# Linear attention into a gated MLP on one core: W_out staged as fp32 on SyncE's queue, half of W_in moved behind step 2, and a new hand-written order

## The chip, the cores and the metric

One core of one Trainium2 chip runs the kernel; the others are idle. The metric is the device time of one execution in microseconds, as a median of several runs. TensorE is called PE here (PEld is its loading of weights), VectorE DVE, ScalarE ACT, GpSimd POOL, and SyncE SP; SP issues nearly all DMAs, all on one queue.

## What is computed

The inputs are q, k and v of shape (4 batches, 8 heads, 768 tokens, 64), a decay per head, and the weights of a gated MLP. All are fp32, and so is the output (4, 768, 512).

```
for each block of 64 tokens b:                      # causal linear attention with decay lam
    out[b]  = (q_b k_b^T * Dmask) v_b + (q_b * lam^(i+1)) @ kv_state
    kv_state = lam^64 * kv_state + (k_b * lam^(63-i))^T v_b
x = out as (batch, token, 512)
h = relu(x @ w_in); u, v = halves of h              # w_in 512 x 1024
v = (v - mean(v)) / sqrt(var(v) + 1e-6)
v = w_spatial @ v + b_spatial                       # mixes the 768 tokens of a batch
y = (u * v) @ w_out                                 # w_out 512 x 512
```

## The kernel before, in words

**Tiles.** The 4 x 768 tokens are cut into 12 steps of 256 tokens, numbered n = 0 to 11, three to a batch. A step is two tiles c = 0, 1 of 128 tokens. Everything on PE is bf16 with fp32 sums in PSUM, of which eight banks are used: seven for work, and bank 7 for the running state of the attention. q, k and v are loaded as fp32 into three buffers each (512 KB a load), the decays are multiplied in while they are turned into bf16 (`qc`, `kc`, two buffers each), and v is cast (`vb`, two buffers). In steps 0 to 4 PE transposes qc and kc and an engine copies the result out of PSUM; from step 5 on SP does it with DMA transposes.

**Order.** The kernel is written as one list of tokens, `ORDER` (L16 to L85). Each token is an operation with its arguments and, last, its engine: T is PE, D is DVE, A is ACT, P is POOL, S is SP. `tc.manual_schedule()` (L570) takes them as they stand, so each engine executes its own tokens strictly in that order, and semaphores between engines follow from the data. A token that waits holds all later tokens of its engine. Engines that appear in the text are therefore a part of the token: `QM.2.0.D` is on DVE and `QM.2.0.P` on POOL. The tokens that the text uses:

| token | what | line |
|---|---|---|
| LQ, LK, LV n | SP loads q, k, v of step n | L195 |
| QM, KM n.x | decay times q or k, half x of the heads' pairs | L316 |
| VC n, VD n.x | cast of v, whole or half | L184 (POOL), L180 (ACT), L182 (DVE) |
| TQ, TK / EQ, EK | PE transposes of q, k / their copy out of PSUM | L351 / L180, L182 |
| DQ, DK n | the same by DMA transpose from SP | L333, L329 |
| SC n.i, MK n.i | scores, half i / times the causal mask | L381, L386 |
| KV n.c, SS n.c | add to the state / copy it out | L398, L180 or L182 |
| AV n.c | attention output of part c (state part and block part) | L419, L428 |
| FN n | one-element read of a bank after AV n.0 | L441 by copy |
| EX n.z | copy of the attention output to xT | L180, L182 |
| PV n.c, EV n.c, BN n.c | x @ w_in for the v half / relu / mean and variance | L453, L458 or L460, L468 and L469 |
| RA, RD, RB, VN | 1/sqrt(var) and the normalising of v | L473, L478, L483, L489 or L492 |
| PU n.j, EU n.j | x @ w_in for the u half / relu | L504, L458 or L460 |
| WT k.i, EW k.i | PE transposes of w_spatial, rows' half i / copy out | L516, L180 or L182 |
| GP, PW, GM b.f.i | bias into a bank / spatial product of batch b / times u | L526, L530, L536 |
| PO b.t, EO, ST | product with w_out, copy out, store of a 128 x 512 tile | L541, copy, L564 |
| PH, EH, SH | the same for half a tile, used for the last one | L550, copy, L560 |
| FL k.w | k matmuls of width w on ones, whose result nobody reads | L299 |

**Stages.** The start holds steps 0 to 2 up to PU, and then WT; for batch b, eight PW need all of the batch's normalised v, and are followed by its six PO, mixed with the attention and the first MLP product of the next batch. GN (L496) is a one-element copy on POOL that only waits for VN 2.1 (and VN 5.0), so that POOL's later tokens start after it.

**Weights.** WH.0 and WH.1 load the v half of w_in as fp32 into the staging buffer `wst[0]`, WH.2 and WH.3 the u half into `wst[1]`; CW.0 to 3 and CX.0 and 1 cast them to bf16. WQ.0 to 5 load the six row blocks of w_spatial (384 KB each) into parts of `wst[0]`, `wss` and `wst[1]`, once the casts have read what was there; WC casts them. WO (L279) is one DMA from POOL's own queue that loads w_out and casts it on the way.

Of the kernel before, what the change touches and what calls it, by code (L numbers as in the profile page):

```python
# [8 lines left out]
FP32 = mybir.dt.float32  # L9
# [7 lines left out]
msk.P one.D idn.P FL.6.256.3.1.T LQ.0.S lam.A BR.A tab.0.A row.D LK.0.S FL.2.256.2.1.T LK.1.S LB.6.T LQ.1.S  # L17
FL.16.128.0.1.T LV.0.S WH.0.S WH.1.S LV.1.S WH.2.S LQ.2.S LK.2.S WH.3.S LV.2.S FL.6.256.2.0.T posk.P mkc.D
LN.6.A LL.D LX.A tab.1.A QM.0.1.D QM.0.0.P KM.0.0.P KM.0.1.D TQ.0.0.3.T TQ.0.1.5.T EQ.0.0.3.D TK.0.0.4.T
EQ.0.1.5.A EK.0.0.4.A KM.1.0.D TK.0.1.0.T BB.1.2.T KM.1.1.D EK.0.1.0.D BE.1.2.A QM.1.0.D SC.0.0.5.6.T TK.1.1.1.T  # L20
FL.2.256.2.0.T SC.0.1.3.4.T TK.1.0.0.T EK.1.1.1.A MK.0.0.5.6.D EK.1.0.0.A TQ.1.0.2.T EQ.1.0.2.A MK.0.1.3.4.D
VC.0.P BB.0.1.T BE.0.1.A KV.0.0.T QM.1.1.P SC.1.0.5.6.T SS.0.0.A MK.1.0.5.6.D AV.0.0.3.4.T FN.0.3.4.A TQ.1.1.2.T
KV.0.1.T EQ.1.1.2.A AV.0.1.3.4.T SS.0.1.A CW.0.P CW.1.P CW.2.P CW.3.P WQ.0.S WQ.1.S WQ.2.S WQ.3.S SC.1.1.0.1.T
eps.D EX.0.0.3.D EX.0.1.4.A MK.1.1.0.1.D VD.1.0.A VD.1.1.P PV.0.0.2.T EV.0.0.2.D PV.0.1.5.T EV.0.1.5.D KV.1.0.T
SS.1.0.A AV.1.0.0.1.T FN.1.0.1.A KV.1.1.T AV.1.1.0.1.T SS.1.1.A BN.0.0.D CX.0.P EX.1.0.0.D EX.1.1.1.A PU.0.0.5.T
EU.0.0.5.A PV.1.0.6.T QM.2.1.P BN.0.1.D QM.2.0.D RA.0.A EV.1.0.6.A TQ.2.1.3.T EQ.2.1.3.A KM.2.0.D PV.1.1.2.T
EV.1.1.2.A TQ.2.0.4.T EQ.2.0.4.A KM.2.1.D TK.2.0.0.T TK.2.1.1.T PU.1.0.5.T EK.2.0.0.D EK.2.1.1.D BN.1.0.D RD.0.D
EU.1.0.5.A CX.1.P WQ.4.S WQ.5.S LQ.3.S LK.3.S LV.3.S SC.2.0.3.4.T SC.2.1.0.1.T PU.0.1.6.T MK.2.0.3.4.D VC.2.P
EU.0.1.6.A MK.2.1.0.1.D RB.0.D KV.2.0.T SS.2.0.A PU.1.1.5.T AV.2.0.3.4.T FN.2.3.4.A EU.1.1.5.A BN.1.1.D
AV.2.1.3.4.T WC.0.P WC.1.P WC.2.P WT.0.0.6.T EX.2.1.4.A EX.2.0.3.D WT.1.0.2.T WT.2.0.0.T EW.0.0.6.D EW.1.0.2.A  # L30
RA.1.A EW.2.0.0.D VN.0.0.D LQ.4.S LK.4.S PV.2.0.1.T EV.2.0.1.A BN.2.0.D PV.2.1.4.T EV.2.1.4.A VN.0.1.A BN.2.1.D
RD.1.D VN.1.0.D VN.1.1.D WC.3.P WC.4.P WC.5.P QM.3.1.P GP.0.0.0.4.A RA.2.A GP.0.2.0.5.A PU.2.0.3.T EU.2.0.3.A
PU.2.1.0.T EU.2.1.0.A WT.0.1.6.T WT.1.1.2.T RD.2.D VN.2.0.D VN.2.1.D EW.0.1.6.D WT.2.1.1.T EW.1.1.2.D EW.2.1.1.D
LV.4.S LQ.5.S LK.5.S GN.2.1.P QM.3.0.P KM.3.1.P KM.3.0.P PW.0.0.0.4.T GP.0.3.1.3.A PW.0.2.0.5.T TQ.3.2.6.T
GM.0.0.0.4.D GP.0.1.0.0.A EQ.3.2.6.A PW.0.3.1.3.T PW.0.1.0.0.T TK.3.2.1.T GP.0.3.0.4.A PW.0.3.0.4.T GM.0.2.0.5.D
GM.0.3.1.3.D GM.0.1.0.0.D EK.3.2.1.D VC.3.A SC.3.0.1.2.T SC.3.1.5.6.T QM.4.0.P QM.4.1.P KM.4.0.P KV.3.0.T
# [52 lines left out]
def kernel(  # L89
# [514 lines left out]
```

## Time and profile before

| | us |
|---|---|
| median of 3 runs | 143.67 (143.55 to 143.78) |
| profiled execution, first to last instruction (span) | 148.0 |
| PE, DVE, ACT, POOL busy in it | 136.3, 113.5, 76.3, 58.1 |

The profile is one execution of its own, taken by the hardware profiler; its only time is its span, and that is longer than the runs without it. Times below are microseconds from the start of that span. PE's busy time is that of pipelined matmuls with modelled ends, so 10 busy microseconds in 10 do not mean that PE streams at its full rate: the rate is read from how far apart groups of matmuls start. The chain of waits follows the work back from the last instruction, at each step to whatever released it; its pieces give start, duration, engine, tile, line and count.

### The profile page before, as it was taken

To read this page: it belongs to the slowest core of one execution; us is meant where nothing else is said; L and a number is where in the kernel's file an instruction comes from. 1 tells how busy PE (TensorE), PEld (TensorE's weight loads), DVE (VectorE), ACT (ScalarE), POOL (GpSimd) and SP (SyncE) were. 2 spreads that over 40 slices of the span, in tenths; PEclk is the share of its full clock that TensorE was granted. 3 is DMA by queue.
4 is the path that set the end of the run, shared out by engine and by line. 5 is a ranking of instruction groups with operands and counts; after the bars stand their busy time and mean duration, and the time that the engine had idled before them with its cause. 6 is when DMAs were issued, how large, how long until landed. Compare 5 with 4: busy or idle time off the path is not lost.

```text
span 148.0 us, 4675 instructions
## 1 busy us (share of the span) xinstructions
PE 136.3 (92%) x1965; PEld 87.4 (59%) x1983; DVE 113.5 (77%) x220; ACT 76.3 (52%) x155; POOL 58.1 (39%) x67
## 2 busy tenths in 40 slices
PE   5979999599999979999999999999999999999990
PEld 3846645377767636565766564776664655856540
DVE  3484669997978858679599959986898989984930
ACT  3564618247973434676921476778508443480040
POOL 5529537970299924398510504904700000000000
PEclk9985579999999999999999999999999999999998
DMA  3999999999969999999898399999987550510174
GB/s 89 346 355 371 352 357 406 367 303 330 326 190 275 125 130 293 334 217 296 184 273 83 80 303 373 241 320 235 198 180 102 190 213 30 187 71 0 39 300 159
DMA packets 58841, 34.12 MB, mean 231 GB/s; under 512 B 15939, under 2 KB 54595, under 8 KB 58820
## 3 DMA queue, kind: packets, MB, share of 16 engines
q1 hardware_dynamic: 58144, 33.17, 82.2%
q0 software_dynamic: 528, 0.52, 2.7%
q8 instruction: 15, 0.25, 0.7%
q10 hardware_dynamic: 148, 0.13, 0.3%
q14 instruction: 6, 0.05, 0.1%
HBM read 24.38 MB, written 6.29 MB: 207 GB/s over the span
## 4 chain that ended last, share of the span: by engine, by line
PE 78%; DVE 8%; ACT 4%; DMA 3%; issue 3%; POOL 2%; POOLq 0%
PE ps L530 20%; PE ps L504 13%; PE ps L453 13%; PE ps L541 13%; PE ps L398 4%; PE ps L381 4%; PE ps L428 4%; DMA q_in<-in_q_dram 3%; PE ps L351 3%; DVE a_sb L386 2%; PE ps L419 2%; DVE kc L316 2%; PE ps L285 2%; PE ps L516 1%; DVE gT L536 1%
## 5 line engine op out<-in xcount | busy, mean ns | idle before, releaser
L386 DVE TENSOR_TENSOR a_sb<-ps,m 128x1024 bf16<-128x1024 f32 x24 | 28.9, 1218 | 6.9 <-PE ps L381 4.5
L530 PE MATMUL ps<-wt_sb,vn 128*128 128x384 bf16 x192 | 33.8, 326 | 0.2 <-ACT ps L180 0.2
L530 PEld LDWEIGHTS <-vn 128*128 128x128 bf16 x192 | 18.2, 98 | 12.5 <-issue 0.4
L316 POOL TENSOR_TENSOR kc<-k_in,lv 128x512 bf16<-128x512 f32 x16 | 17.4, 1097 | 20.4 <-DMA k_in<-in_k_dram 8.3
L453 PE MATMUL ps<-win_sb,xT 128*128 128x512 bf16 x87 | 22.8, 393 | 1.0 <-DVE xT L182 0.4
L504 PE MATMUL ps<-xT,win_sb 128*128 128x256 bf16 x192 | 23.5, 273 | 0.0
L316 POOL TENSOR_TENSOR qc<-q_in,lqn 128x512 bf16<-128x512 f32 x19 | 20.4, 1090 | 4.6 <-DMA q_in<-in_q_dram 4.5
L536 DVE TENSOR_TENSOR gT<-ps,uT 128x384 bf16<-128x384 f32 x32 | 16.8, 550 | 6.9 <-PE ps L530 3.8
L541 PE MATMUL ps<-wout_sb,gT 128*128 128x512 bf16 x83 | 21.2, 379 | 0.7 <-issue 0.5
L504 PEld LDWEIGHTS <-win_sb 128*128 128x128 bf16 x192 | 18.1, 98 | 3.9
L468 DVE BATCH_NORM_STATS2 st<-vh 128x6 f32<-128x512 bf16 x24 | 16.3, 681 | 1.5 <-ACT vh L458 1.4
L458 ACT ACTIVATE vh<-ps 128x512 bf16<-128x512 f32 x19 | 11.4, 598 | 9.2 <-PE ps L453 9.2
L180 ACT ACTIVATE o_sb<-ps 128x512 f32<-128x512 f32 (+1 forms) x17 | 9.6, 570 | 12.2 <-DVE o_sb L182 8.9
L453 PEld LDWEIGHTS <-xT 128*128 128x128 bf16 x96 | 9.2, 101 | 10.9 <-issue 1.4
L541 PEld LDWEIGHTS <-gT 128*128 128x128 bf16 x92 | 8.6, 98 | 9.0 <-DVE gT L536 0.2
L458 ACT ACTIVATE uT<-ps 128x512 bf16<-128x512 f32 x17 | 9.8, 588 | 5.0 <-PE ps L504 5.0
L398 PEld LDWEIGHTS <-kc 64*64 64x64 bf16 x320 | 7.1, 113 | 7.2 <-issue 5.6
L180 ACT ACTIVATE ps<-bsp 128x384 f32<-128x384 f32 x21 | 10.0, 488 | 2.4 <-DVE a_sb L386 1.2
L428 PE MATMUL ps<-a_sb,vb 64*64 64x128 bf16 x384 | 11.2, 225 | 0.0
L180 ACT ACTIVATE xT<-ps 128x512 bf16<-128x512 f32 x16 | 9.1, 594 | 4.1 <-PE ps L428 3.9
L184 POOL CAST vb<-v_in 128x1024 bf16<-128x1024 f32 (+1 forms) x7 | 6.8, 976 | 10.7 <-DMA v_in<-in_v_dram 5.5
L180 ACT ACTIVATE s_sb<-ps 128x256 bf16<-128x256 f32 x15 | 5.7, 380 | 10.3 <-PE ps L398 10.2
(69 smaller groups left out, 181.8 us busy)
## 6 DMA issues: line engine op xcount, KB each, us to landing
q_in<-in_q_dram SPq DMA_DIRECT2D x12, 512.0 KB, 7.0
k_in<-in_k_dram SPq DMA_DIRECT2D x12, 512.0 KB, 6.1
v_in<-in_v_dram SPq DMA_DIRECT2D x12, 512.0 KB, 6.1
out_dram<-o_sb SPq DMA_DIRECT2D x23, 256.0 KB, 2.6
wst<-in_moe_w_in_dram SPq DMA_DIRECT2D x4, 512.0 KB, 6.6
wst<-in_moe_w_spatial_dram SPq DMA_DIRECT2D x4, 384.0 KB, 6.1
wss<-in_moe_w_spatial_dram SPq DMA_DIRECT2D x2, 384.0 KB, 6.3
wout_sb<-in_moe_w_out_dram POOLq DMA_DIRECT2D x1, 512.0 KB, 5.9
```

What stands on the lines that cost most here:

```text
L180: nc.scalar.activation(out=o, in_=i, func=AF.Copy)
L316: vec(e).tensor_tensor(out=dst[n % NCA][:, u].rearrange("p u m o d -> p o (u m) d"), in0=src[n % NIN].rearrange("p (o u) m d -> p o u m d" ...
L386: nc.vector.tensor_tensor(out=a_sb[n % NA][:, i].rearrange("p o w j x -> p o w (j x)"), in0=ps[:, b0:b1 + 1:b1 - b0].rearrange("p o (w y) ...
L398: nc.tensor.matmul(out=pkv[row(o), u], lhsT=kc[n % NCA][row(c), u, m, o, :], rhs=vb[n % NCA][row(c), 4 * o + u, m, :], start=new and u == ...
L428: nc.tensor.matmul(out=po[c ^ o][row(w), c, i], lhsT=vb[n % NCA][row(c), 4 * o + u, j, :], rhs=a[row(c), i, o, w, j, :], start=(r == 0 and ...
L453: nc.tensor.matmul(out=bank(b), lhsT=x[:, slot(c, g)], rhs=win_sb[:, g, DH:DFF], start=(g == 0), stop=(g == NCH - 1))
L458: nc.scalar.activation(out=o, in_=i, func=AF.Relu)
L468: nc.vector.bn_stats(out=st6[p2][:, t], in_=vh[p2][:, t])
L504: nc.tensor.matmul(out=pu[:, f2].rearrange("p (c x) -> p c x", c=2), lhsT=win_sb[:, g, f * P:(f + 1) * P], rhs=x[:, slot(0, g):slot(1, g) ...
L530: nc.tensor.matmul(out=bank(b)[:, 0:HW], lhsT=vn[bb % 2][:, s, f * P:(f + 1) * P], rhs=wt_sb[:, s, i * HW:(i + 1) * HW], start=False, stop ...
L536: nc.vector.tensor_tensor(out=gT[bb % 2][:, f, cols], in0=bank(b)[:, 0:HW], in1=uT[bb % 2][:, f, cols], op=ALU.mult)
L541: nc.tensor.matmul(out=bank(b), lhsT=gT[bb % 2][:, f, t * P:(t + 1) * P], rhs=wout_sb[:, f, :], start=(f == 0), stop=(f == NCH - 1))
```

## The change

Three things change at once.

1. **w_out** is no longer loaded by POOL's queue. SP loads it as fp32 (1 MB) into `wst[0]` behind step 4's keys (`WP`), and POOL casts it in two instructions of 128 x 1024 (`WX.0`, `WX.1`).
2. **The u half of w_in** (`WH.2`, `WH.3`) is loaded behind step 2's q and k, no longer WH.2 ahead of them and WH.3 behind them. The row blocks of w_spatial come in the order 2, 1, 0, 3, 5, 4.
3. **All orders are new**, and many tokens change their engine. `brow`, the bias row, is now the first row of `bsp`. The new functions for a state kept in two banks (`KP`, `SX`, `SY`, `SA`), `FX` and `BQ` are not used by the new order.

```diff
-    brow = sb([1, S], FP32, "brow")
+    brow = bsp[0:1]
...
+    def w_p(e):
+        nc.sync.dma_start(out=wst[0], in_=moe_w_out.rearrange("(t p) f -> p t f", p=P))
+
+    def w_x(e, j):
+        copy(e, wout_sb[:, 2 * j:2 * j + 2], wst[0][:, 2 * j:2 * j + 2])
```

The start of the order, engine by engine, before (-) and after (+), fillers left out of DVE and ACT:

```diff
-SP   LQ.0 LK.0 LK.1 LQ.1 LV.0 WH.0 WH.1 LV.1 WH.2 LQ.2 LK.2 WH.3 LV.2 WQ.0 .. WQ.5 LQ.3 LK.3 LV.3 LQ.4 LK.4 LV.4 LQ.5 LK.5 LV.5 LK.6 LV.6 DQ.5 DK.5
+SP   LQ.0 LK.0 LK.1 LQ.1 LV.0 WH.0 WH.1 LV.1 LQ.2 LK.2 WH.2 WH.3 LV.2 WQ.2 WQ.1 WQ.0 WQ.3 WQ.5 WQ.4 LQ.3 LK.3 LV.3 LQ.4 LK.4 WP LV.4 LK.5 LQ.5 LK.6 LV.5 DK.5 DQ.5
-POOL QM.0.0 KM.0.0 VC.0 QM.1.1 CW.0 CW.1 CW.2 CW.3 VD.1.1 CX.0 QM.2.1 CX.1 VC.2 WC.0 .. WC.5 QM.3.1 GN.2.1 QM.3.0 KM.3.1 KM.3.0 QM.4.0 QM.4.1 KM.4.0 KM.4.1 WO QM.5.1 QM.5.0 KM.5.0 KM.5.1 VC.4 KM.6.0
+POOL QM.0.0 KM.0.0 KM.1.0 QM.1.0 QM.1.1 KM.1.1 CW.3 CW.2 QM.2.0 KM.2.1 KM.2.0 CX.1 VC.2 WC.2 WC.1 WC.5 WC.4 QM.3.1 GN.2.1 KM.3.1 VC.3 QM.4.1 QM.4.0 KM.4.1 KM.4.0 WX.0 WX.1 VC.4 QM.5.0 QM.5.1 KM.6.1
-DVE  QM.0.1 KM.0.1 EQ.0.0 KM.1.0 KM.1.1 EK.0.1 QM.1.0 MK.0.0 MK.0.1 MK.1.0 EX.0.0 MK.1.1 EV.0.0 EV.0.1 BN.0.0 EX.1.0 BN.0.1 QM.2.0 KM.2.0 KM.2.1 EK.2.0 EK.2.1 BN.1.0 RD.0 MK.2.0 MK.2.1 RB.0 BN.1.1 EX.2.0 EW.0.0
+DVE  QM.0.1 KM.0.1 EQ.0.0 EK.0.1 BE.0 EQ.0.1 MK.0.0 MK.0.1 EK.1.0 CW.1 SS.0.0 FN.0 EQ.1.0 BE.1 EX.0.1 MK.1.0 MK.1.1 EV.0.1 BN.0.1 QM.2.1 EV.0.0 BN.0.0 EK.2.0 MK.2.1 EV.1.0 MK.2.0 BN.1.1 BN.1.0 FN.2 RD.0 WC.0 RB.0
-ACT  EQ.0.1 EK.0.0 BE.1 EK.1.1 EK.1.0 EQ.1.0 BE.0 SS.0.0 FN.0 EQ.1.1 SS.0.1 EX.0.1 VD.1.0 SS.1.0 FN.1 SS.1.1 EX.1.1 EU.0.0 RA.0 EV.1.0 EQ.2.1 EV.1.1 EQ.2.0 EU.1.0 EU.0.1 SS.2.0 FN.2 EU.1.1 EX.2.1
+ACT  EK.0.0 VC.0 EQ.1.1 CW.0 EK.1.1 EX.0.0 SS.0.1 VD.1.1 VD.1.0 SS.1.0 FN.1 EX.1.0 EX.1.1 EQ.2.0 EQ.2.1 EK.2.1 CX.0 EV.1.1 RA.0 SS.1.1 EU.1.1 SS.2.0 EU.1.0 EU.0.0 RA.1 EX.2.0 EX.2.1 EU.0.1
-PE   .. PV.0.0 PV.0.1 KV.1.0 AV.1.0 KV.1.1 AV.1.1 PU.0.0 PV.1.0 TQ.2.1 PV.1.1 TQ.2.0 TK.2.0 TK.2.1 PU.1.0 SC.2.0 SC.2.1 PU.0.1 KV.2.0 PU.1.1 AV.2.0 AV.2.1 WT.0.0 WT.1.0 WT.2.0
+PE   .. PV.0.0 PV.0.1 KV.1.0 AV.1.0 AV.1.1 TQ.2.0 PV.1.0 TQ.2.1 TK.2.1 PV.1.1 TK.2.0 SC.2.1 KV.1.1 SC.2.0 PU.1.0 PU.0.0 PU.1.1 KV.2.0 AV.2.0 PU.0.1 AV.2.1 WT.1.0 WT.2.0 WT.0.0
```

From the first WT to the first PW of batch 1, DVE has 61 tokens after and 56 before; among them the decays KM.3.0, QM.3.0, KM.5.0, KM.5.1, KM.6.0 (before: QM.6.1 and KM.8.0). Batch 0's first PO stands ahead of step 3's PV after, and behind step 4's first AV before. The end of the order:

```diff
-PE   PW.3 x7 PO.3.0 PW.3.3.1 PO.3.2 PO.3.4 PO.3.1 PO.3.3 PH.3.5.0 PH.3.5.1
+PE   PW.3 x8 PO.3.1 PH.3.5.1 PH.3.5.0 PO.3.2 PO.3.3 PO.3.4 PO.3.0
```

The last copy and store are that of half a tile before, and of a whole tile (`EO.3.0` on ACT, `ST.3.0` on SP) after.

More of the change, by code (lines that the diff above doesn't have):

```diff
@@ L16 @@
 ORDER = """
[L17 to L36, printed above, removed]
@@ L82 @@
[L82 to L84 removed]
+LQ.0.S LK.0.S LK.1.S LQ.1.S LV.0.S WH.0.S WH.1.S LV.1.S posk.P msk.P idn.P row.D one.D lam.A BR.A tab.0.A
+FL.6.256.1.1.T FL.2.256.3.1.T FL.2.256.3.1.T LB.5.T FL.16.128.3.1.T FL.6.256.4.1.T mkc.D LN.5.A LL.D LX.A QM.0.1.D
+QM.0.0.P TQ.0.0.5.T KM.0.1.D TK.0.1.3.T EQ.0.0.5.D EK.0.1.3.D KM.0.0.P BB.0.0.T TK.0.0.5.T TQ.0.1.1.T KM.1.0.P
@@ L172 @@
     wss = sb([P, 2, S], FP32, "wss")
+    ysb = many(2, [P, 4 * D], FP32, "ysb") if " KP." in ORDER else None
     wst = many(2, [P, NCH, DH], FP32, "wst")
@@ L299, in f_l, with f_x @@
             nc.tensor.matmul(out=bank(b)[:, 0:w], lhsT=ones[:, 0:P], rhs=ones[:, 0:w],
+                             start=(new == 1 and i == 0), stop=True, skip_group_check=True)
+    def f_x(e, k, w, new):
+        for i in range(k):
+            nc.tensor.matmul(out=bank(SB)[:, 4 * D:4 * D + w], lhsT=ones[:, 0:P], rhs=ones[:, 0:w],
                              start=(new == 1 and i == 0), stop=True, skip_group_check=True)
```

137 lines of the change are left out of this document (87 added, 50 removed).

## The prediction

> **What bounds the kernel now.** I read the page first, then a table by stages, then the timeline of the start.
>
> ```profile
> span 148.0 us, 4675 instructions
> PEclk9985579999999999999999999999999999999998
> PE 78%; DVE 8%; ACT 4%; DMA 3%; issue 3%; POOL 2%; POOLq 0%
> ```
>
> The chain that ends last is PE for 78% of 148.0. The other 22% is where time can be found. The table by stages (columns: stretch, length, busy PE, PEld, DVE, ACT, POOL with counts, granted clock, DMA share, GB/s) tells where it lies:
>
> ```profile
> 6.80:10.20 3.40, 2.55 (x40) 1.64 (x39) 3.02 (x6) 1.62 (x3) 1.42 (x1) 1.00 1.15 346
> 10.20:20.40 10.20, 9.62 (x145) 5.83 (x144) 5.95 (x8) 4.85 (x11) 6.96 (x9) 0.50 1.10 362
> 20.40:33.50 13.10, 10.84 (x234) 7.33 (x233) 11.87 (x20) 6.59 (x15) 9.12 (x9) 1.00 1.04 355
> 33.50:72.50 39.00, 37.27 (x583) 24.99 (x580) 31.33 (x65) 24.86 (x51) 23.37 (x25) 1.00 1.08 248
> 72.50:100.90 28.40, 28.14 (x451) 17.97 (x453) 23.48 (x48) 16.27 (x35) 9.02 (x9) 1.00 0.96 237
> 100.90:130.40 29.50, 29.02 (x426) 18.22 (x429) 26.57 (x53) 14.90 (x32) 4.53 (x4) 1.00 0.62 159
> ```
>
> From 33.5 on PE is idle for little: 1.7, 0.3 and 0.5 in the three stretches. What PE has to stream there does not change, and takes these pieces of the chain (start, length, engine, line, count):
>
> ```profile
> 39.24 1.95 PE ps L530 x12
> ...
> 72.92 3.90 PE ps L530 x24
> ...
> 84.05 3.45 PE ps L541 x16
> ...
> 89.96 2.59 PE ps L453 x12
> ...
> 97.65 3.49 PE ps L504 x32
> ...
> 115.39 0.45 PE ps L381 x32
> ...
> 130.75 6.99 PE ps L530 x42
> ```
>
> So a PW costs 0.98 (1.95 for two), a PO 0.86, a PV 0.86, a PU 0.87, a score half 0.22. Batch 1's first PW stands near 72.5, batch 3's near 130.4. Ahead of 33.5 it is otherwise: the clock is 0.50 from 10.2 to 20.4, and from 20.4 to 33.5 DVE is busy for 11.87 of 13.10 while the queue moves 355 GB/s. That is the stage of this change, and its timeline says which wait ends last:
>
> ```profile
> 5.14 0.69 DVE L316 TENSOR_TENSOR qc<-q_in,lqn 128x512 bf16<-128x512 f32 x1 [0.68 <-DMA q_in<-in_q_dram]
> ...
> 17.77 1.04 POOL L184 CAST win_sb<-wst 128x1024 bf16<-128x1024 f32 x1 [0.51 <-DMA wst<-in_moe_w_in_dram]
> ...
> 17.97 1.89 PE L453 MATMUL ps<-win_sb,xT 128*128 128x512 bf16 x4 [0.37 <-DVE xT L182]
> ...
> 19.28 1.04 POOL L316 TENSOR_TENSOR qc<-q_in,lqn 128x512 bf16<-128x512 f32 x1 [0.47 <-DMA q_in<-in_q_dram]
> ...
> 22.08 1.04 POOL L184 CAST win_sb<-wst 128x1024 bf16<-128x1024 f32 x1 [1.76 <-DMA wst<-in_moe_w_in_dram]
> ...
> 24.13 1.04 POOL L184 CAST vb<-v_in 128x1024 bf16<-128x1024 f32 x1 [1.01 <-DMA v_in<-in_v_dram]
> ...
> 24.16 1.55 DVE L316 TENSOR_TENSOR qc<-q_in,lqn 128x512 bf16<-128x512 f32 x1
> ...
> 25.64 2.53 DVE L316 TENSOR_TENSOR kc<-k_in,lv 128x512 bf16<-128x512 f32 x2
> ...
> 27.00 0.40 PE L351 MATMUL ps<-ident,kc 128*128 128x128 bf16 x4 [0.83 <-DVE kc L316]
> ...
> 28.23 0.40 PE L351 MATMUL ps<-ident,kc 128*128 128x128 bf16 x4 [0.83 <-DVE kc L316]
> ...
> 28.46 1.04 PE L504 MATMUL ps<-xT,win_sb 128*128 128x256 bf16 x8
> ...
> 33.58 1.18 PE L516 MATMUL ps<-ident,wsp_raw 128*128 128x128 bf16 x18
> ```
>
> Step 2's three decays on DVE run from 24.16 to 28.17, though q had landed by 19.28. PE waits for each (0.83, 0.83), and steps on only at 28.46. Beside POOL's casts such a decay takes 1.27 to 1.55, alone 0.69 (at 5.14).
>
> **The change part by part.** Durations that I need besides:
>
> ```profile
> L316 POOL TENSOR_TENSOR kc<-k_in,lv 128x512 bf16<-128x512 f32 x16 | 17.4, 1097 | 20.4 <-DMA k_in<-in_k_dram 8.3
> L386 DVE TENSOR_TENSOR a_sb<-ps,m 128x1024 bf16<-128x1024 f32 x24 | 28.9, 1218 | 6.9 <-PE ps L381 4.5
> L180 ACT ACTIVATE xT<-ps 128x512 bf16<-128x512 f32 x16 | 9.1, 594 | 4.1 <-PE ps L428 3.9
> L180 ACT ACTIVATE vb<-v_in 128x1024 bf16<-128x1024 f32 x3 | 3.2, 1050 | 0.0
> L468 DVE BATCH_NORM_STATS2 st<-vh 128x6 f32<-128x512 bf16 x24 | 16.3, 681 | 1.5 <-ACT vh L458 1.4
> ```
>
> *Queue.* From WH.2 (17.77) to q 2 (19.28) a 512 KB load takes 1.5. With both u quarters behind step 2's q and k, q 2 is usable at 17.8, k 2 at 19.3, the first quarter at 20.8, the second and v 2 at 22.1 and 24.1 as before.
>
> *Steps 0 and 1.* v 0 is cast on ACT, so POOL takes step 1's keys and queries. Both score halves of step 0 stand together, and their masks follow back to back on DVE (1.22 each, from about 10.1 to 12.5; before there is a gap). I get the end of AV.0.1 at 14.7 and the first PV at 16.0, 2.0 ahead of 17.97. At half clock a PV takes about 1.7: both end at 19.4. Then KV, AV, a state copy and AV: 20.9. Now something else is late: both EX of step 1 are on ACT, 0.59 each one behind the other, so PV.1.0 waits till 22.25.
>
> *Step 2.* Three of four decays are on POOL at 1.1: 17.8 to 18.9, 19.3 to 21.5; the fourth is on DVE behind step 0's statistics, done at 22.6 if it takes as long as at 24.16. The transposes therefore interleave with PV.1.0 and PV.1.1 and end at 24.7, not 28.6. Scores: 24.75 and 25.5.
>
> *u half.* `CX.0` sits on ACT behind EK.2.1, from 24.6 for 1.05 (the row of vb, same size): the first PU starts at 25.7, not after a landing. From there four PU (3.9 with their edges), KV (16 matmuls) and AV (48), 0.9 by the score halves' 0.22 for 16, give 30.5. `WC.0` is on DVE behind two statistics (0.9 each with their sum) and the read that waits for AV.2.0.
>
> ```profile
> L182 DVE CAST vb<-v_in 128x1024 bf16<-128x1024 f32 x2 | 1.5, 744 | 0.0
> ...
> L182 DVE COPY qT<-ps 128x512 bf16<-128x512 bf16 x1 | 0.4, 425 | 0.0
> ```
>
> DVE has no cast of 128x768 in the trace. From below it is bounded by the copy of 512 columns, 0.42, from above by the decay beside POOL, 1.55; I take 0.7, since the cast of 1024 at 0.74 is the nearest row. Done at 30.95, so **WT starts at 31.0 instead of 33.58: -2.6.**
>
> *First WT to batch 1's first PW.* PE has three WT, 2 PV, 2 PU, three WT (5.7 in all), then 30.5 to batch 1's first PW. I walked all four engines through it and find waits of 1.85: 0.2 for the bias copy of the third PW behind QM.3.0, 0.2 before SC.3.0, 0.25 where `KM.5.1` and `KM.5.0` stand ahead of MK.4.1, 0.55 where MK.5 comes behind `KM.6.0`, 0.4 for both EX of step 5 on ACT, 0.25 in smaller ones. That is 38.05. Before it took 39.0 with 0.2 more PE work in it: **-0.7.** DVE does not bound it: its 56 operations before sum to 34.5 at their mean durations and show 31.33 busy, because neighbours overlap; the 61 after sum to 37.7, by the same ratio 34.2, under PE's 36.2. (The heavy kinds are alike: 6 MK, 8 GM, 8 statistics, 9 VN. What differs is 5 decays for 2 and 3 relus of v for none, against 2 EW for 5.)
>
> *w_out.* What goes is one issue on POOL:
>
> ```profile
> L279 POOL DMA_DIRECT2D wout_sb<-in_moe_w_out_dram x1 | 0.9, 931 | 0.0
> ```
>
> WP takes 3.0 (twice a 512 KB load). After v 2 (24.1) come six w_spatial blocks (384 KB, 1.1 each) and five inputs (1.5 each), 38.2, so w_out is usable at 41.2, or 42.3 if WQ.5 has to wait for `CX.0` on ACT. POOL reaches `WX` at 43.5 and needs 2 x 1.04. The first PO then comes at 48.8, so 3.3 of cover; the POOL issue that goes was not on the path. What WP delays on SP (v 4, k 5, q 5, k 6, v 5) is usable at 44.9 (v 4), 46.5 (k 5), 48.1 (q 5); k 5 is wanted by DVE at 48.5. Cost 0; if the queue were 2 later, DVE's MK.4.1 behind KM.5 would pay it one for one.
>
> *DMA transposes.* DK.5 can be issued when KM.5.0 is done, 50.5. Landing takes 4.0:
>
> ```profile
> kT<-kc SPq DMA_TRANSPOSE x7, 4.0
> ```
>
> DQ.5 follows it, 57 to 58, and step 5's scores come at 58.3. Further on DK.8 and DQ.8 stand behind KV.6.1, which the new order moves behind five PW; they land between 1.0 ahead of the scores of step 8 and 1.2 behind. I take **+0.3** for both.
>
> *Batches 1 to 3.* From batch 1's first PW to batch 3's PE does the same work but for the 0.2; I find 1.3 of waits, as there are now (57.8 for 56.5): **0**, bounds -0.5 and +1.2.
>
> *Tail.* Before, the last work is two half copies and stores; after, a whole tile.
>
> ```profile
> 143.03 0.97 PE ps L550 x8
> 144.02 0.38 ACT o_sb L180
> ```
>
> A whole copy is 0.2 longer (0.59 to 0.38), a 256 KB store 0.4 longer than one of 128 KB at the loads' rate, and of the two half copies one waits for the other now, which goes: **+0.5.**
>
> Sum: -2.6 - 0.7 + 0.3 + 0 + 0.5 = -2.5. The profiled span would be 145.5. The span lies 4.3 above the median, in both kernels alike as I suppose; so 143.67 - 2.5 = **141.2**.
>
> **The rivals.** *B, the clock returns one window sooner.* The table has the clock at 0.50 for 10.2, three times 3.4, so it is decided by stretches of 3.4. If 13.6 to 17.0, where PE now starts PV.0.0, counts as busy, both PV end at 18.2, not 19.4, and WT starts at 29.5. Time 139.8.
>
> *C, the clock falls once more.* From 6.8 to 10.2 PE is busy 2.55 of 3.40, and the next stretch is at 0.50. From 20.4 to 23.8 the new order has, by my walk, about 2.3 busy, with the wait for PV.1.0 in it. At half clock the 3.0 of PE work in the next 3.4 would cost 2.5. Time 143.7. The Trainium skill, "TensorE: Matmul & The Clock Gate", section "What's actually happening", has the gate decided by free-running windows of about 3.4 us, half rate after an idle one and full after a busy one. The trace agrees with the length (10.2 in three); where "busy" begins, no row here shows.
>
> *D, DVE becomes the bound (slower).* POOL and DVE hold each other up: 1.27 to 1.55 against 0.69 for one decay. After, five decays sit on DVE in the stage from WT to batch 1, beside POOL's own, before two. If operations there do not overlap, the 37.7 and 2.5 to 3 of waits make 40.7 instead of 38.05, and batches 2 and 3, with the same mixture, give 0.6 each more: +2.7 + 1.2 on top of 141.2, **145.1**. It decides once DVE's work in the stage is over PE's 36.2. Against it: 31.33 busy for 34.5. The Trainium skill, "SBUF — State Buffer", section "Who interferes with whom", makes the port pair that DVE and GpSimd share an exclusive lock when a DVE operation has two SBUF inputs; the decays have, and 1.55 against 0.69 agrees with it.
>
> *E, no gain.* WT waits for w_spatial anyway: if the last block is late because WQ.5 must wait for `CX.0` on ACT (25.6), the rest of the queue shifts by 1 and the start's gain is lost in POOL and DVE later. 143.7.
>
> **How the numbers follow.** Forecast 0.50, B 0.15, C 0.13, D 0.17, E 0.05. The forecast's own spread is 1.0 either way. The range runs from 139.3, just under B, to 145.1, half of D. A measurement of this kernel tells about 0.2% from no change, 143.4 to 144.0: that takes half of C and most of E, 0.09. Slower is D and the upper edge of E and C, 0.19. Faster is the rest, 0.72.
>
> **What would show it.** Right: the first w_spatial transposes on PE near 31, batch 1's first PW near 69, batch 3's near 127.5; PE waits for kc of step 2 gone; the first PV near 16. B and C: the granted clock between 10 and 27. D: DVE busy over 34 between WT and batch 1, and PE's waits there for a_sb and kc. Wrong: a wait of PE for w_out, or POOL's `WX` waiting for a landing past 46; a later first PW of batch 1 than 72.5.

## The result and the profile after

| | us |
|---|---|
| before, median of 4 runs beside it | 143.72 (143.55 to 143.94) |
| after, median of 4 runs | 151.4 (148.91 to 155.41) |
| ratio, 95% interval | 1.042 (1.034 to 1.051) |
| profiled execution of after: time, span | 155.41, 153.7 |

The change made the kernel 4% slower where the prediction had it 1.7% faster, and its runs differ by 6.5 where those of before differ by 0.4. Ratios here and below leave out the runs marked slow on record: of after 148.91 and 151.01 count, while the median of all four lies 5% above before. The page of after (span, two rows of the 40 slices, granted clock, GB/s, and the chain of waits by engine):

```profile
span 153.7 us, 4672 instructions
PE   5989989989500999999999999999999999999991
DVE  3569787999999799698787998999489789876850
PEclk9995699999995699999999999999999999999999
GB/s 106 344 368 364 348 342 355 344 315 341 364 183 0 196 83 4 148 293 344 336 186 223 210 129 275 348 317 217 239 240 76 85 303 302 6 0 273 0 203 207
PE 78%; DVE 17%; issue 2%; ACT 1%; DVEq 0%
```

The twelfth and thirteenth slice of PE (42 to 50) are empty, which no slice of before was but the very last; DVE is at 9 (tenths busy) in them; from there on the DMAs move little for five slices (183, 0, 196, 83, 4), and the clock drops to 0.5 a second time. DVE's share of the chain went from 8% to 17%. One wait is behind it (PE's two longest waits for another engine between 30 and 79: engine, line, waited for, total, times, longest):

```profile
PE ps L363 <- DVE kc L328: 9.4, 1, 9.4
PE ps L541 <- DVE vh L497: 0.8, 1, 0.8
```

The timeline from 37.5 on, all engines (start, length, engine, line, operation, tiles, shapes, count, idle time ahead):

```profile
37.54 0.68 DVE L328 TENSOR_TENSOR qc<-q_in,lqn 128x512 bf16<-128x512 f32 x1
37.69 0.58 POOL L533 CAST seen<-vn 1x1 f32<-1x1 bf16 x1 [4.78 <-DVE vn L529]
...
38.23 1.03 POOL L328 TENSOR_TENSOR kc<-k_in,lv 128x512 bf16<-128x512 f32 x1
38.68 11.07 DVE L328 TENSOR_TENSOR kc<-k_in,lv 128x512 bf16<-128x512 f32 x1
39.21 1.03 POOL L182 CAST vb<-v_in 128x1024 bf16<-128x1024 f32 x1
...
40.21 2.03 POOL L328 TENSOR_TENSOR qc<-q_in,lqn 128x512 bf16<-128x512 f32 x2
42.21 2.03 POOL L328 TENSOR_TENSOR kc<-k_in,lv 128x512 bf16<-128x512 f32 x2
44.19 2.01 POOL L182 CAST wout_sb<-wst 128x1024 bf16<-128x1024 f32 x2
46.16 1.03 POOL L182 CAST vb<-v_in 128x1024 bf16<-128x1024 f32 x1
47.16 2.03 POOL L328 TENSOR_TENSOR qc<-q_in,lqn 128x512 bf16<-128x512 f32 x2
...
49.80 1.04 PE L363 MATMUL ps<-ident,kc 128*128 128x128 bf16 x8 [9.39 <-DVE kc L328]
```

`KM.3.0.D`, which takes 0.68 alone (`QM.3.0.D`, the same size, at 37.54), is counted as busy for 11.07. In that time POOL runs eleven instructions one behind the other, each starting 0.03 to 0.05 before the one ahead ends: `KM.3.1` (already under way), `VC.3`, `QM.4.1`, `QM.4.0`, `KM.4.1`, `KM.4.0`, `WX.0`, `WX.1`, `VC.4`, `QM.5.0`, `QM.5.1`, to 49.19. DVE ends 0.55 behind the end of the last of them. Nothing stops that row but itself: PE waits for DVE, ACT for PE, and POOL goes on until its own next decay needs a buffer that PE has to free.

**A second trace** of the same kernel (141.8, span 140.1) shows what it does without that. DVE asks at the same point of the row and is let in behind POOL's second instruction, 2.11 in all:

```profile
34.63 1.03 POOL L328 TENSOR_TENSOR kc<-k_in,lv 128x512 bf16<-128x512 f32 x1
...
35.08 2.11 DVE L328 TENSOR_TENSOR kc<-k_in,lv 128x512 bf16<-128x512 f32 x1
35.62 1.03 POOL L182 CAST vb<-v_in 128x1024 bf16<-128x1024 f32 x1
...
36.62 1.48 POOL L328 TENSOR_TENSOR qc<-q_in,lqn 128x512 bf16<-128x512 f32 x1
```

A new trace of before (143.82, span 142.1) stands beside it. In both new traces, time less span is 1.7, as for after (155.41 and 153.7). The profile of before that the prediction worked with had a span of 148.0 and PE at half clock from 10.2 to 20.4 (mean clock 0.961); the runs of before listed with a clock since then had 0.993 to 1.0, so that one execution was some 6 longer than the median it was set against.

By stages (start to first WT; to batch 1's first PW; to batch 3's; to the end), before and then after, both at full clock up to after's tail (0.96):

```profile
0.00:27.38 27.38, 24.24 (x447) 16.92 (x447) 20.97 (x38) 15.99 (x33) 16.82 (x27) 1.00 1.00 330
27.38:66.68 39.30, 37.77 (x587) 25.02 (x581) 31.20 (x65) 24.97 (x51) 24.76 (x27) 1.00 1.19 284
66.68:124.51 57.83, 57.83 (x881) 36.14 (x880) 50.09 (x100) 31.10 (x66) 14.71 (x15) 1.00 0.84 204
124.51:142.10 17.59, 13.72 (x79) 7.45 (x77) 9.12 (x18) 3.97 (x8) 0.00 (x0) 1.00 0.32 120
```

```profile
0.00:28.14 28.14, 23.89 (x446) 16.59 (x446) 21.13 (x43) 15.71 (x30) 17.05 (x25) 1.00 0.99 325
28.14:65.39 37.25, 37.14 (x572) 24.84 (x564) 33.84 (x67) 26.09 (x50) 22.00 (x22) 1.00 1.10 289
65.39:123.33 57.94, 57.94 (x897) 36.46 (x896) 49.87 (x100) 31.30 (x65) 18.63 (x19) 1.00 0.78 209
123.33:140.10 16.77, 13.37 (x80) 7.53 (x77) 9.22 (x19) 4.14 (x9) 0.00 (x0) 0.96 0.41 156
```

The same stages of the trace of 155.41, the second and third being up to the decay and the decay itself:

```profile
0.00:30.09 30.09, 26.91 (x444) 19.09 (x446) 21.52 (x42) 15.71 (x30) 17.90 (x26) 0.89 0.98 321
30.09:38.68 8.59, 7.62 (x79) 5.41 (x73) 8.41 (x19) 6.87 (x13) 3.30 (x5) 1.00 1.10 331
38.68:49.75 11.07, 1.73 (x16) 1.10 (x14) 11.07 (x3) 1.60 (x3) 10.51 (x11) 0.81 0.57 181
```

### The profile page after: what moved, and what is told of

Its sections match the earlier page's. It is cut to its first block, busy times and chain, and to the rows that moved or that the text cites. A ratio compares the mean times of both kernels' runs of the same rounds, so it can differ in the third digit from the quotient of the medians.

```text
span 153.7 us, 4672 instructions
## 1 busy us (share of the span) xinstructions
PE 135.6 (88%) x1968; PEld 88.5 (58%) x1983; DVE 124.6 (81%) x225; ACT 77.4 (50%) x152; POOL 57.4 (37%) x66
## 4 chain that ended last, share of the span: by engine, by line
PE 78%; DVE 17%; issue 2%; ACT 1%; DVEq 0%
PE ps L567 19%; PE ps L578 13%; PE ps L490 12%; PE ps L541 11%; DVE kc L328 7%; PE ps L393 4%; PE ps L465 4%; PE ps L306 4%; PE ps L363 3%; PE ps L410 3%; PE ps L456 2%; DVE vn L529 2%; DVE st L505 2%; DVE a_sb L398 2%; PE ps L292 1%
## 5 line engine op out<-in xcount | busy, mean ns | idle before, releaser
L328 POOL TENSOR_TENSOR kc<-k_in,lv 128x512 bf16<-128x512 f32 x18 | 19.0, 1066 | 30.9 <-PE ps L410 21.2
L328 POOL TENSOR_TENSOR qc<-q_in,lqn 128x512 bf16<-128x512 f32 x21 | 22.0, 1065 | 15.8 <-DMA q_in<-in_q_dram 10.6
L178 ACT ACTIVATE o_sb<-ps 128x512 f32<-128x512 f32 (+1 forms) x14 | 7.9, 582 | 16.6 <-PE ps L578 16.6
L328 DVE TENSOR_TENSOR kc<-k_in,lv 128x512 bf16<-128x512 f32 x6 | 14.8, 2480 | 0.4 <-DMA k_in<-in_k_dram 0.4
L178 ACT ACTIVATE xT<-ps 128x512 bf16<-128x512 f32 x20 | 11.2, 595 | 6.7 <-PE ps L465 6.4
L495 ACT ACTIVATE uT<-ps 128x512 bf16<-128x512 f32 x20 | 11.4, 591 | 2.6 <-PE ps L541 2.6
L363 PE MATMUL ps<-ident,kc 128*128 128x128 bf16 x40 | 4.3, 252 | 9.4 <-DVE kc L328 9.4
L178 ACT ACTIVATE kT<-ps 128x512 bf16<-128x512 bf16 (+1 forms) x5 | 3.8, 767 | 16.0 <-PE ps L363 16.0
L393 PE MATMUL ps<-qT,kT 64*64 64x128 bf16 x384 | 10.3, 226 | 0.5 <-DVE eps_t L210 0.5
L465 PE MATMUL ps<-a_sb,vb 64*64 64x128 bf16 x384 | 10.4, 224 | 0.0
```

The source lines that it names most:

```text
L178: nc.scalar.activation(out=o, in_=i, func=AF.Copy)
L328: vec(e).tensor_tensor(out=dst[n % NCA][:, u].rearrange("p u m o d -> p o (u m) d"), in0=src[n % NIN].rearrange("p (o u) m d -> p o u m d" ...
L393: nc.tensor.matmul(out=pa[o][row(c), w, j], lhsT=kT[n % NTR][row(o), u, j, c * Q64:(c + 1) * Q64], rhs=qv(n, o, u, c), start=(w == 0 and j ...
L465: nc.tensor.matmul(out=po[c ^ o][row(w), c, i], lhsT=vb[n % NCA][row(c), 4 * o + u, j, :], rhs=a[row(c), i, o, w, j, :], start=(r == 0 and ...
L495: nc.scalar.activation(out=o, in_=i, func=AF.Relu)
```

## The experiments

**Theory 1**: DVE's decay, both inputs in SBUF, needs something that POOL holds while it computes from SBUF (the port pair of rival D), and a row of POOL instructions, one behind the other without a gap, keeps it. **Theory 2**: the wait is for data. **Theory 3**: the new orders are longer anyway, and the stall only hides it.

**The decay on POOL.**

```diff
- DVE  .. QM.3.0.D GP.0.0.0.D KM.3.0.D ..     POOL .. GN.2.1.P KM.3.1.P ..
+ DVE  .. QM.3.0.D GP.0.0.0.D ..              POOL .. GN.2.1.P KM.3.0.P KM.3.1.P ..
```

> After, with KM.3.0 alone moved from DVE to POOL, directly ahead of KM.3.1. Theory 1 (the decay KM.3.0 on DVE could not get at the memory while POOL ran eleven instructions without a gap, 38.2 to 49.2): the 9.4 us in which PE waits for kc of step 3 go, TK.3.2.1 starts at about 40.4, one POOL decay (1.0) later than a smooth KM.3.0 would let it, and the time is 143.5 to 145.5, with little spread between runs. Theory 2 (the wait is for data: keys of step 3 that land late, or a buffer that comes free late, and the engine doesn't matter): the wait stays near 10 and the time at 149 to 155. Theory 3 (the new orders are longer anyway, the stall only hides it): the stall goes, but the time stays over 147.

Measured 141.95 (141.34 to 143.41), ratio to before 0.988 (0.982 to 0.995). One decay moved gives back the whole loss and more. That is on theory 1's side, and lower than the 143.5 that it had named at least. Theory 3 falls.

**The decay stays on DVE, POOL is made to pause.**

```diff
+    def after_kc(e, n):
+        nc.gpsimd.tensor_copy(out=seen, in_=kc[n % NCA][0:1, 0, 0, 0, 0:1])
- POOL .. GN.2.1.P KM.3.1.P VC.3.P ..
+ POOL .. GN.2.1.P KM.3.1.P GK.3.P VC.3.P ..
```

> After, with KM.3.0 left on DVE, and one tiny POOL instruction added behind KM.3.1 that reads one element of the half of kc that KM.3.0 writes, so that POOL has to wait until DVE is done. Work is added, none is taken away. Theory 1: POOL pauses at 39.3, DVE gets through within 0.6 of it, KM.3.0 takes 1.0 to 1.3 instead of 11.1, and the time falls by 4 to 10 to 143.5 to 146. Theory 2 (late data): POOL waits as long as DVE, everything behind it is later, the time is 151 or longer.

Measured 143.17 (141.62 to 144.48), ratio 0.985 (0.980 to 0.991) from 141.62 and 141.92; the other two runs lie at 144.4 and 144.5, with mean clocks of 0.971 and 0.988, and why is open. The timeline of the 141.62 around the gate:

```profile
34.62 1.03 POOL L328 TENSOR_TENSOR kc<-k_in,lv 128x512 bf16<-128x512 f32 x1
...
35.08 1.13 DVE L328 TENSOR_TENSOR kc<-k_in,lv 128x512 bf16<-128x512 f32 x1
...
36.34 0.18 POOL L536 CAST seen<-kc 1x1 f32<-1x1 bf16 x1 [0.69 <-DVE kc L328]
```

POOL stands still for 0.69, DVE ends 0.56 behind `KM.3.1`, and an added wait makes the kernel faster than after by 8. Late data would have made it no faster, and `KM.3.1` reads the same load of k and ran at 38.23 in the trace of after: theory 2 falls.

**The same decay on DVE in the kernel before.**

```diff
- POOL .. GN.2.1.P QM.3.0.P KM.3.1.P KM.3.0.P ..
+ POOL .. GN.2.1.P QM.3.0.P KM.3.1.P ..         DVE  + KM.3.0.D at that place
```

> The kernel before, with KM.3.0 alone moved from POOL to DVE, in the same place of the order; w_out still by POOL's own queue. Theory 1: KM.3.0 starts on DVE beside POOL's row of decays (39.9 to 46.0 without a gap) and ends only when POOL pauses, at the w_out issue near 46 or, if that keeps the port too, near 51: PE waits for kc of step 3 from about 44 on, the time is 145 to 151 and differs between runs. Theory 2 or 3: nothing in this kernel changes but one decay of 0.7 on DVE instead of 1.0 on POOL, 143.2 to 144.2.

Measured 143.74 (143.38 to 144.98), ratio 1.000 (0.997 to 1.003). Theory 1 in this plain form failed here: the decay got in behind the POOL instruction under way, in 1.47, as the prediction had it.

```profile
34.78 1.03 POOL L316 TENSOR_TENSOR kc<-k_in,lv 128x512 bf16<-128x512 f32 x1
...
34.89 1.47 DVE L316 TENSOR_TENSOR kc<-k_in,lv 128x512 bf16<-128x512 f32 x1
...
35.78 1.49 POOL L316 TENSOR_TENSOR qc<-q_in,lqn 128x512 bf16<-128x512 f32 x1
```

So a row of POOL does not always shut DVE out.

**w_out by POOL's queue, decay on DVE.** After, with one issue in the place of the two casts:

```diff
- SP .. LK.4.S WP.S LV.4.S ..     POOL .. KM.4.0.P WX.0.P WX.1.P VC.4.P ..
+ SP .. LK.4.S LV.4.S ..          POOL .. KM.4.0.P WO.P VC.4.P ..
```

> After, with w_out loaded and cast by POOL's own queue again (one issue of 0.9 in the place of the two casts of 1.0, and no load on SP). KM.3.0 stays on DVE. Theory 1: POOL's row from KM.3.1 on is broken by the issue at about 44.2, DVE gets in there at the latest, the stall is 5 to 6 at most, the time 144 to 148.5. If an issue keeps the port as well: like after, 149 to 155. If w_out on SP is the cause by itself: no stall, 141 to 143.

Measured 149.94 (147.71 to 150.25); the times alone do not tell it from after.

```profile
35.81 7.04 DVE L327 TENSOR_TENSOR kc<-k_in,lv 128x512 bf16<-128x512 f32 x1
...
39.34 2.03 POOL L327 TENSOR_TENSOR kc<-k_in,lv 128x512 bf16<-128x512 f32 x2
41.32 0.93 POOL L276 DMA_DIRECT2D wout_sb<-in_moe_w_out_dram  x1
42.25 1.48 POOL L181 CAST vb<-v_in 128x1024 bf16<-128x1024 f32 x1
```

The decay ends at 42.85, 0.60 behind the end of the issue, and the cast behind it takes 1.48 instead of 1.03. The time is in the range named for an issue that keeps DVE out, and while the issue ran it did; but the row ends there as theory 1 had it, since DVE got in at the end of the issue with POOL's next instruction ready. The stall of 7 is longer than the 5 to 6 named, because the issue ran first. w_out on SP is not the cause by itself, as the stall is there without it; that its two casts lengthen the row is read from the timeline of after.

**Rows of POOL by themselves.** Four kernels of nothing but stretches, each built on what the one ahead had shown. *From standstill* means that POOL had waited ahead of the row; the end of a POOL instruction is called open if a DVE instruction that waits gets in there, and shut if POOL's next one comes first.

> No part of the reference is computed: the output is a constant, and the kernel consists of stretches in which POOL runs 10 ready instructions (decays of 128 x 512, or casts of 128 x 1024) in a row and DVE gets one instruction during the first of them; each stretch waits for the one ahead. Kinds on DVE: a decay (two inputs in SBUF) beside decays, three times; beside casts, twice; four decays in a row; a decay beside three; then beside casts one tensor_scalar, one cast of 128 x 1024, one product with an input in PSUM, one tiny instruction 128 x 2, one VN form; a tensor_scalar beside decays; and last 12 decays on DVE with 4 on POOL begun during the first. Theory 1: the decay on DVE takes up to 10 us and ends 0.6 after POOL's last, at least in some stretches; beside three it takes 3; with one SBUF input or a PSUM input it takes its own 0.4 to 0.7. Rival (the two take turns, as at 24 to 28 us of the trace of before): the decay on DVE takes 1.3 to 1.6 in every stretch.

In this kernel each POOL instruction waited for the one ahead (all wrote to one place), with a gap of 0.06 to 0.08 between them, and DVE got in at the first gap every time: a decay took 0.87 to 1.55, and the decays in rows took turns with POOL's. With the input in PSUM the product took its own 0.56. The one-input forms waited too: the cast of 128 x 1024 took 1.50, the tensor_scalar 1.22. Theory 1 got the kinds wrong there.

> As the kernel of stretches before (no part of the reference is computed), but POOL's nine instructions of a stretch write nine different places, so that none waits for the one ahead and they follow without a gap, as in the stall. DVE's decay is asked for at different moments of POOL's first one, by a copy from PSUM of 0, 64, 128 ... 512 columns ahead of it. Theory 1a (a row of POOL instructions without a gap never lets go of the port): every DVE decay lasts until POOL's row ends, 8 to 9.5 us. Theory 1b (between two POOL instructions there is a short moment, and DVE gets it or not by the phase): some stretches take 1.0 to 1.6 and some several us, by the delay. Rival (they take turns always, the stall has another cause): 1.0 to 1.6 in all.

Without gaps, DVE's decay took 8.9 to 9.3 in five stretches with decays on POOL and 0.8 to 1.2 in six, in turn; beside rows of casts it took 4.9 to 5.5 in all three, to the row's end. The moment of asking within the instruction made no difference. What differed in the rows of decays: a row that follows another without standstill shut DVE out, one ahead of which POOL had waited did not.

> Stretches as before (no part of the reference is computed): five POOL decays without a gap behind one tiny instruction that POOL has waited for, so that the row starts from standstill; DVE asks in the middle of the first, second, third or fourth of them, twice each. Then twice a row that follows another row without standstill, asked in the first and in the third; twice 9 casts of 128 x 512 asked at the start; last, asked in the third, one tiny two-input instruction and one tensor_scalar with one input. Rule R (only the end of an instruction that POOL began from standstill is open to DVE): asked in the first 1.0 to 1.2; in the second 4.1, in the third 3.1, in the fourth 2.1, always 0.55 behind the row's end; without standstill 5 and 3.1. Rival (chance or phase): short and long ones mixed, the two rounds differ. One-input tensor_scalar: 0.7 by Theory 1.

POOL's row with the ask in its second instruction, then DVE's decay (`xo`) asked in the second, third and fourth of a row from standstill, and in the first of a row without it:

```profile
59.39 5.49 POOL L548 TENSOR_TENSOR wsp_raw<-k_in,lv 128x512 bf16<-128x512 f32 x5
...
60.91 1.06 DVE L548 TENSOR_TENSOR xo<-k_in,lv 128x512 bf16<-128x512 f32 x1
...
70.62 1.01 DVE L548 TENSOR_TENSOR xo<-k_in,lv 128x512 bf16<-128x512 f32 x1
...
81.27 2.02 DVE L548 TENSOR_TENSOR xo<-k_in,lv 128x512 bf16<-128x512 f32 x1
...
95.01 5.05 DVE L548 TENSOR_TENSOR xo<-k_in,lv 128x512 bf16<-128x512 f32 x1
```

The second to the fourth agree in both rounds to 0.01: no chance in it (the very first row started late). In the first of a row from standstill it took 1.05, in the third of a row without it 3.01. Rule R failed for the second and third, which were open; the fourth was shut. The rows of casts gave one of each, 5.48 and 1.06, both from standstill; of the two asked in the third, the tiny two-input instruction took 0.48 and the one-input tensor_scalar 0.74.

> Stretches as before (no part of the reference is computed), rows of POOL decays that start from standstill: asked in the third of 4, the fourth of 9, the sixth of 9, the third of 9, the fourth of 7, then fourth and sixth of 9 again. If the end of the row decides (the last one can't be passed): third of 4 takes 1.5, and in the rows of 9 the next end is open, 1.0 each. If the time since standstill decides (open till about 3.2, shut from 4.2): 1.0 for every third, and to the row's end for the fourth and sixth: 5.5 and 3.5 of 9, 3.5 of 7. Last two stretches: a row without standstill with a memset, or an iota, amid its second part, asked in the second of three ahead of it: if an instruction of POOL that reads nothing in SBUF lets DVE in, it ends 0.55 behind the second or third decay, 1.5 to 2.5, else at the row's end, 5 or more.

Asked in the fourth: 6.02 of 9 (twice) and 4.02 of 7; in the sixth 3.97 and 3.98 of 9, all to the row's end; in the third of 9, 1.01. (The third of 4 came out as the fourth, the kernel's first row being late, and says nothing.) So a row of such decays from standstill was open up to the third instruction and shut from the fourth, in rows of 5, 7 and 9. The last two stretches:

```profile
145.81 3.05 DVE L548 TENSOR_TENSOR xo<-k_in,lv 128x512 bf16<-128x512 f32 x1
148.26 0.51 POOL L568 MEMSET x<- 128x512 bf16 x1
...
160.52 6.15 DVE L548 TENSOR_TENSOR xo<-k_in,lv 128x512 bf16<-128x512 f32 x1
162.98 0.12 POOL L570 IOTA poski<- 128x6 int32 x1
```

A memset on POOL lets DVE in: it ends at 148.86, 0.55 behind the decay ahead of the memset. An iota of 0.12 does not. Each was run once.

**The same two kernels again.**

> The kernel before once more, for a trace at a time near its median (the profile that the prediction used had a span of 148.0 and a mean clock of 0.961). Expected: a span of about 142, no stretch at half clock between 13 and 24, the first w_spatial transposes on PE earlier than 33.57 by about 5, and the same order of waits after it.

> The changed kernel once more, for a second trace. Theory 1: KM.3.0 on DVE ends again about 0.55 behind the last of POOL's row, 10 to 11 long. If the stall is the same each time, the spread of the times (148.91 at a mean clock of 0.986, 155.41 at 0.956) comes from the clock that falls while PE waits, not from the stall's length. If the length is chance, 4 to 11.

143.82 and 141.8: the traces shown above. Before's first WT stood at 27.38, 6.2 earlier than in the first profile. After had no stall, against every length that was expected; one run could not say which is the rule.

> The changed kernel in more runs. If the stall is a race that falls one way or the other: two groups of times, one near 141.8 (clock near 1.0) and one from 148 on (clock 0.956 to 0.988), little between. If it hangs on the chip or on that first set of runs alone: all near 141.8.

Measured 142.63, 147.6, 148.28, 151.18, 152.59, 153.7: one without and five with. With the others, nine of eleven runs of this kernel lie at 147.6 or above, two at 141.8 and 142.63, nothing between. The trace of this set (151.18) has the decay at 9.05; it ended 0.54 behind the instruction after which POOL paused 0.18 for q of step 5. So the stall's length varies (11.07, 9.05), and the mean clock is lower where the time is longer, though not in step: 155.41 and 153.7 had mean clocks of 0.956 and 0.942, 147.6 and 148.91 of 0.988 and 0.986, but 148.28 has 0.962.

**The decay stays on DVE and asks 0.5 earlier.**

```diff
- DVE  .. QM.3.0.D GP.0.0.0.D KM.3.0.D ..
+ DVE  .. QM.3.0.D KM.3.0.D GP.0.0.0.D ..
```

> After, with KM.3.0 left on DVE but asked for 0.5 earlier, directly behind QM.3.0 and ahead of a copy (GP.0.0.0); nothing else moves. If it matters at which moment DVE asks (behind QM.3.0 the two engines take turns, as at 24 to 28 in the trace of before): KM.3.0 takes 1.3 to 2, no stall in any run, 141.5 to 143. If POOL's row shuts DVE out at any moment: stalls as in after, 148 to 155 in most runs.

Measured 142.06 (141.62 to 142.73), ratio 0.986 (0.981 to 0.990), no run near 147.

```profile
34.48 0.69 DVE L328 TENSOR_TENSOR qc<-q_in,lqn 128x512 bf16<-128x512 f32 x1
...
34.63 1.18 POOL L533 CAST seen<-vn 1x1 f32<-1x1 bf16 x1 [1.58 <-DVE vn L529]
...
35.08 0.69 DVE L328 TENSOR_TENSOR kc<-k_in,lv 128x512 bf16<-128x512 f32 x1
```

KM.3.0 takes 0.69, not the 1.3 to 2 expected: it follows QM.3.0 at once, and POOL's `GN.2.1` waits for both. Swapping two neighbours on DVE is enough: DVE then asks ahead of POOL's row and not inside it.

> The version with KM.3.0 on POOL in more runs: the race can't fall the wrong way there. 141.3 to 142.5 in nearly all, median 141.8, none over 145.

142.28 (141.79 to 143.4), ratio 0.988 (0.983 to 0.993): as expected.

**The other two parts, in the version with the decay on POOL.** w_out by POOL's queue, in the casts' place and early (behind `QM.3.1`):

> The version with KM.3.0 on POOL (141.95), with w_out by POOL's own queue again: the w_out part undone, without the stall. The prediction costed that part at nothing: 141.6 to 142.4. If w_out on SP costs through what it delays there (v 4, k 5, q 5): 141.0 to 141.5. If its removal from POOL's queue is worth the issue and its packets: 142.5 to 143.

147.6 (144.48 to 148.01), outside all three: a badly placed undo. The issue stood at the casts' place, and its data took 6.5 to land; PE waited 2.5 for w_out. The rest of the 5.6 above its base was not taken apart.

> The version with KM.3.0 on POOL, with w_out by POOL's own queue, issued early, behind QM.3.1 where POOL stands idle, so that it is there when PE wants it (in the version with the issue in the casts' place PE waited 2.5 for w_out and more for what came late behind it). By the prediction's 0 for this part: 141.5 to 142.5. If w_out on SP is worth something by what SP's queue or the packets do: over 142.7.

141.53 (141.51 to 143.58), ratio 0.985 (0.981 to 0.989). Issued early, w_out by POOL's queue costs the same as by SP's, within what the intervals tell.

```diff
- SP .. LQ.2.S LK.2.S WH.2.S ..
+ SP .. WH.2.S LQ.2.S LK.2.S ..
```

> The version with KM.3.0 on POOL (141.95), with the third quarter of w_in loaded ahead of step 2's queries and keys again: that part undone, the orders kept. q 2 and k 2 come 1.5 later. The prediction has the start's gain in the early keys of step 2: PE waits for kc of step 2 again, WT is 1.0 to 1.5 later, 143.0 to 143.5. If the gain is in the orders: 141.8 to 142.2.

144.33 (143.54 to 145.21), ratio 1.004 (0.999 to 1.010): 1.6% lost against the 0.988 of its base. PE waits 1.6 for qc of step 2, and WT starts at 30.70 in place of 28.13. The u half behind step 2's keys is worth 2.3 in this order, more than expected. Not all of it is the wait: the granted clock was 0.50 from 21 to 23 in this trace, and all four runs have mean clocks of 0.987 or 0.988 where those of the base have 0.996 to 1.0.

## Why the prediction was wrong

- **The step that failed: the price of a decay on DVE beside POOL.** The prediction took 1.27 to 1.55 for it, from 24 to 28 in before, where the two take turns, used 1.55 as the upper bound, and in rival D charged DVE's sum (5 decays for 2) against PE's. The runs show that 1.5 is the price where POOL lets go, and the rest of POOL's row where it doesn't: 7.04, 9.05 and 11.07 in three traces of this place (the 7.04 without w_out's casts). D was right about the resource and the stage, and priced it as throughput (2.7 and 1.2) when it is latency: one instruction held, with PE behind it. D's sign, DVE over 34 between WT and batch 1, came out as 44.4 busy in the trace of 155.41, but 10.4 of that is the held decay. The walk's "0.2 before SC.3.0" became 9.4. Its bound should have been the length of POOL's row from `KM.3.1` on, eleven instructions in the new order.
- **The page's rule.** The Trainium skill, "SBUF — State Buffer", section "SBUF: two separate sides", has whichever starts first, a DVE operation with two SBUF inputs or a GpSimd operation that reads SBUF, hold the port pair for its whole instruction. The 0.55 to 0.60 from POOL's end to DVE's agrees, and so does the memset, which reads nothing in SBUF; the iota, which reads nothing there either, let nothing in. Who comes next the rule does not say: here the one that waited was passed over up to ten times.
- **The 155.41, added up** from the two traces of after, by the first weight loads of each group: first WT 30.09 for 28.14, 1.95 in a start at lower clock (0.89); WT to the first PW 0.9; to batch 0's first PO (59.55 for 45.95) 10.7 more; after that nothing. Together 13.6, which is 155.41 - 141.8.
- **The base was unusual.** "The span lies 4.3 above the median, in both kernels alike as I suppose" is wrong, and so is the sentence ahead of the prediction that the span is longer than the runs: spans lie 1.7 below the times, and that execution of before was a long one. The mean clock near 1.0 in the runs of before took the ground from rivals B and C: the half clock is no fixed part of the start.
- **Without the stall the sum is right, and its terms are not**; that it fits is luck. Forecast -2.5 in all; the two traces at full clock differ by 2.0, the versions with the decay on POOL (w_out as in after, or issued early) or asked earlier by 1.8 to 2.5 against the runs of before beside them.

| stage | forecast | full clock | why |
|---|---|---|---|
| to the first WT | -2.6 | +0.8 | 27.38 and 28.14; PE's waits for kc were 0.83 twice in the first profile; in the new trace of before PE waits 0.6 for one |
| to batch 1's first PW | -0.7 | -2.1 | PE idle 1.5 before, 0.1 after; the walk's waits of 1.85 did not come |
| batches 1 to 3, with the DMA transposes | +0.3 | +0.1 | |
| tail | +0.5 | -0.8 | last matmul 13.3 and 12.9 behind that PW, 4.3 and 3.9 from there to the end; not taken apart |

- **Right:** the order of the start in that execution (first PV's weights 16.85 for 16.0, PV.1.0 21.66 for 22.25, first PU 25.22 for 25.7, WT 30.09 for 31.0), the 0 for w_out, and its own sign of error: batch 1's first PW came at 78.99, later than 72.5. The times named for v 4, k 5 and q 5 do not follow from the prediction's own sum for the queue, which gives 42.7 for v 4; v 4 landed at 43.6 in the second trace of after.

**Open.** What shuts a row. Rows of equal decays were open for three instructions after a standstill; in the kernel's own row the boundary behind `KM.3.1` was shut in all four traces of after and its w_out variant, and the next one open in one of them. In that one POOL's queue had been held for v 3 until 0.1 ahead of DVE's request; in the other three v 3 had landed earlier, and the queue had passed that wait 0.9 ahead of the request. That how far POOL's queue has run ahead decides it fits these, but no run here took it alone. The landings in the traces narrow it. This decay got in, without an added wait, at 36.65 in the second trace of after and at 35.81 in before with the decay on DVE; the data that POOL's next instruction needed (q 4) had landed only 0.12 and 0.37 ahead of these ends. At the ends of that row that were shut, in the four traces, such data had been there for 0.7 (v 3, in the second trace of after) or for 1.1 and more. So it may be that an end is shut once POOL's next instruction has been ready for some time; this too is argued from few cases, and the memset and the issue are outside it.

## What to carry to other kernels

A DVE instruction with two inputs in SBUF can wait for a whole row of POOL instructions, not for one: before moving one there, count POOL's instructions without a wait behind the place, and take their sum as the upper bound. Where the value is on the path, keep the pair on one engine, let DVE ask ahead of the row, or put a wait into POOL's row; each of the three ended the stall here. And compare a profile's span with the runs' times and clocks before building on it: this one was 6 off, in the very stage that the forecast gained in.

## What was not expected of the hardware

- A 0.68 instruction held 11.07 by another engine, shown as busy time, not as a wait; in other runs gaps of 0.06 to 0.08 between POOL's instructions, 0.18 of pause, the end of an issue or a memset let such an instruction in.
- The same kernel on the same inputs ran at 141.8 to 142.6 or at 147.6 to 155.4; exchanging two neighbours on DVE ended that.
- The stall of 9.4 on PE cost 10.7 by batch 0's first PO: in the trace of 155.41 the granted clock was 0.50 from 47.6 to 51.0 and 0.79 from there to 54.4, just as PE came back.
